# A gated layer whose first two token groups are computed by halves of the hidden units, with 13 instead of 20 weight pieces prepared inside the experts' runs

## The chip, the cores and the metric

The kernel runs on one core of one Trainium2 chip. The metric is the time of one execution on the device in microseconds (us). In the rows of the profile PE is TensorE (its matmuls), PEld its weight loads, DVE is VectorE, ACT is ScalarE, POOL is GpSimd, and SP is the engine that only issues transfers here.

## The reference

Three layers follow each other on 4 x 768 = 3072 tokens of 320 features, all in float32 (the weights of the third layer arrive as float64). The first is an attention with a recurrent state, the second a mixture of 8 experts with one expert per token, the third a gated layer over all tokens:

```
h = np.maximum(x[mask] @ w1[e], 0.0)              # expert e: 320 -> 1024
out[mask] = gate_w[mask, None] * (h @ w2[e])      # 1024 -> 320
...
gate = 1.0 / (1.0 + np.exp(-(x @ w_gate)))        # 320 -> 1536
val = x @ w_val                                   # 320 -> 1536
return (gate * val @ w_out).astype(np.float32)    # 1536 -> 320
```

## The kernel before

Each matrix product is made of parts: a number is split into a high part (rounded for the matmul's format, written by ACT) and a low part (the rest, a subtraction), and the products high x high, high x low and low x high are added up in PSUM. The order of all instructions is written out by hand; every engine works off its own queue in that order.

**The experts.** They are done in nine runs over columns of tokens: runs 0 and 1 are expert 0 (256 + 256 columns), runs 2 to 8 are the other seven with 512, 480, 448, 416, 384, 352 and 336 columns. A run has 8 steps f, one for each block of 128 hidden units (`expert_run`). In a step PE makes the first product of block f (8 matmuls into `h_ps`), ACT writes its high part `hh`, DVE its low part `hl` (L1014, L1015), and PE makes the second product of block f - 2 (8 matmuls into `y_ps`, L935 to L940), which needs `hh` and `hl` of that block. At the end of a run PE transposes the token rows of the next run (`tp_m`, L912) in three parts, each of which ACT and DVE turn into `xh` and `xl` (L210); the transposes have two banks of PSUM. Meanwhile (`expert_steps`) POOL and ACT split the next expert's weights, and three further kinds of work are hung into the steps of runs 2 to 8:

- **weight pieces of the gated layer** (`glu_piece`, `f64_load`, `f64_split`): w_gate and w_val are cut into 20 pieces of 128 rows x 384 units: for each of four stretches of 384 units (three blocks of 128) two of w_gate, two of w_val, and one that holds the last 64 rows of both. A piece is loaded by SP into one of two buffers `raw`, and turned from float64 to a high and a low part: on DVE L1076, L1079, L1082, then (after an ACT instruction, L1085) L1086, L1089 and L1071, which is done twice for the pieces of the last 64 rows (`wgs`, `wvs`). A step with an even f takes up a piece: its first three DVE instructions stand behind step f, the others behind step f + 1. `piece_load` puts the next load into SP's queue when a piece is done.
- **deferred small work** (`defer`): one instruction per step, for offsets, places of the output rows, and flags (`flag_ops`).
- `scale_rows`: the gate weights.

**The gated layer.** 6 groups of 512 tokens (g) times 12 blocks of 128 units (f) are 72 tiles, done group by group. Tile t: PE makes gate and value of (g, f) (`gated_l1`: 16 matmuls with 512 columns, into two of the banks 0, 1, 2, 6); ACT takes the sigmoid (L1527), DVE multiplies (`sgm`, L1528), ACT writes the high part `hh` (L1530), POOL the low part `hl` (L1532); and PE makes the output product of tile t - 2 (`gated_l2`: 12 matmuls with 320 columns into `o_ps`, banks 3, 4, 5, 7, which add up over the 12 blocks of a group). Behind the last tile of a group ACT and DVE copy the four banks out (`gated_out`, L1556, L1558) and POOL scatters them to the output. The layer's 12 pieces of w_out (`wo_load`, 128 x 320) are prepared in the tiles 0 to 11, one each; `due` numbers say before which tile a piece must stand in the queues at the latest (`piece_due`). `group_x` splits the tokens of the next group.

Of the kernel before, what the change touches and what calls it, by code (L numbers as in the profile page):

```python
# [15 lines left out]
ALU = mybir.AluOpType  # L16
# [6 lines left out]
def kernel(  # L23
# [30 lines left out]
    G4 = 4  # L54
# [26 lines left out]
    def tp_ps(name):  # L81
        return next_bank((6, 7), name)
# [1112 lines left out]
    def flag_ops():  # L1195

        v = nc.vector
        fl = const.tile([P, 5], F32, name="fl")
        fb = const.tile([P, 1], BF16, name="fb_")
        ok = const.tile([P, 2, NTILE], F32, name="ok")  # L1200
        we = const.tile([P, 3, NE], F32, name="we")
        z = lambda j: fl[:, j:j + 1]
        ps = {}
        ss = v.tensor_single_scalar

        def total():
            ps[0] = tp_ps("fl_ps")
            nc.tensor.matmul(ps[0][:, 0:1], ones_bf, fb, start=True, stop=True)

        def of_expert(u):  # L1210
            return [
                lambda: v.tensor_tensor(
                    out=vm, in0=pick.rearrange("p k e -> p e k"), in1=by_k(win[:, u]), op=ALU.mult
                ),
                lambda: v.tensor_reduce(out=we[:, u], in_=vm, axis=AX.X, op=ALU.add),
            ]

        return of_expert(0) + of_expert(1) + [
            lambda: v.tensor_tensor(out=we[:, 2], in0=cnt, in1=we[:, 0], op=ALU.is_gt),
            lambda: v.tensor_reduce(out=z(4), in_=we[:, 2], axis=AX.X, op=ALU.max),  # L1220
            lambda: v.tensor_reduce(out=z(3), in_=cnt, axis=AX.X, op=ALU.add),
        ] + block_ops(cnt) + [
            lambda: v.tensor_copy(we[:, 0], nblk),
            lambda: v.tensor_tensor(out=nblk, in0=we[:, 0], in1=we[:, 2], op=ALU.mult),
            lambda: v.tensor_reduce(
                out=z(0), in_=ri_all.rearrange("p c s -> p (c s)"), axis=AX.X, op=ALU.max
            ),
            lambda: ss(out=z(0), in_=z(0), scalar=RLIM, op=ALU.is_gt),
            lambda: ss(out=ok[:, 0], in_=ssq, scalar=1e-9, op=ALU.is_ge),
            lambda: ss(out=ok[:, 1], in_=ssq, scalar=1e30, op=ALU.is_le),  # L1230
            lambda: v.tensor_tensor(out=ok[:, 0], in0=ok[:, 0], in1=ok[:, 1], op=ALU.mult),
            lambda: v.tensor_reduce(out=z(1), in_=ok[:, 0], axis=AX.X, op=ALU.add),
            lambda: ss(out=z(1), in_=z(1), scalar=float(NTILE), op=ALU.is_lt),
            lambda: v.tensor_tensor(out=fb, in0=z(0), in1=z(1), op=ALU.add),
            total,
            lambda: v.tensor_scalar(
                out=z(2), in0=z(3), scalar1=float(NT), scalar2=None, op0=ALU.not_equal
            ),
            lambda: v.tensor_tensor(out=z(2), in0=ps[0][:, 0:1], in1=z(2), op=ALU.add),
            lambda: v.tensor_scalar_min(z(2), z(2), 1.0),  # L1240
            lambda: v.tensor_tensor(out=flags[:, 0:1], in0=z(4), in1=z(2), op=ALU.max),
            lambda: v.tensor_copy(flags[:, 1:2], z(2)),
            lambda: v.tensor_scalar(out=z(2), in0=z(2), scalar1=-1.0, scalar2=1.0, op0=ALU.mult, op1=ALU.add),
            lambda: v.tensor_scalar_mul(nlow, we[:, 1], z(2)),
        ]


    last_part = []

    def expert_steps(n):  # L1250

        k = runs[n][0]
        more = n + 1 < len(runs)
        run_ = expert_run(n)

        acts, rest, ends, loads = ([[] for _ in range(NF1)] for _ in range(4))

        def refill(f, u, e, p, lo=None):

            if e < NE:  # L1260
                copies, lows = (split_w1, split_w2)[u](e, p, lo)
                acts[f] += copies
                rest[f].append(lows)
                e, p = (e, p + 2) if p < 2 else (e + 1, p - 2)
                if e < NE:
                    loads[f].append(lambda: (load_w1, load_w2)[u](e, p))

        def prepare(f):
            if n == 1:
                if f % 2:  # L1270
                    refill(f, 0, 1, f // 2)
                elif f == 4:
                    refill(f, 1, 1, 0, nc.vector)
            else:
                if blanks:
                    acts[f].append(blanks.pop(0))
                if f % 2:
                    refill(f, 1, k + f // 4, (f // 2 + 2) % 4)
                elif f or k > 1:
                    refill(f, 0, k + (f > 0), (f // 2 + 3) % 4)  # L1280
                else:
                    refill(f, 1, 1, 1, nc.vector)
                rest[f].append(defer[0:1])
                del defer[0:1]
                if f % 2 == 0:
                    acts[f] += last_part
                    a, b, c, last_part[:] = piece() if (f == 4 if n == 2 else f < 6 or n < 5) else ([],) * 4
                    rest[f].append(a)
                    acts[f + 1] += b
                    ends[f + 1] += c  # L1290
            if 3 <= f < 7 and n > 1 and more:
                acts[f] = scale_rows(n + 1)[f - 3:f - 2] + acts[f]
            if f == 6 and n == 2:
                acts[f] += diag_ops(n)
            if f == 2 and n == 2:
                acts[f] += diag_ops(0) + diag_ops(1)
            if f == 4 and n == 2:
                ends[f].append(scale_first)

        for f in range(NF1):  # L1300
            next(run_)
            if f == 0 and more:
                load_x(n + 1)
            prepare(f)
            if n == 1:
# [12 lines left out]
        return run_
# [126 lines left out]
            for c0 in range(0, F2, NW)  # L1445
        ), key=lambda z: (z[2], z[1]),
    )
    todo = [(z[2] // P, lambda z=z: glu_piece(*z)) for z in todo]
    ready = []

    def piece_load():
        if todo:
            due, load = todo.pop(0)
            ready.append((due, load()))

# [34 lines left out]
    piece_load()  # L1490
    piece_load()
    blanks = [blank(j) for j in range(8)]
    defer = offset_ops() + place_ops() + flag_ops()

    for n in range(2, len(runs)):
        next(expert_steps(n), None)
    weave(last_part)


    NG = NTILE // G4  # L1500
    last = NG * NF2 - 1
    wo = {}

# [8 lines left out]
        return lambda: f64_split(t, DM, [(whole, wo[f][0])], [(whole, wo[f][1])])  # L1512

    load_wo()
    todo += [(f + 2, lambda f=f: wo_load(f)) for f in range(NF2)]
    todo.sort(key=lambda z: z[0])
    while len(ready) < 2:
        piece_load()
    hs, os_ = {}, {}

    def gated_l1(t):
        g, f = t // NF2, t % NF2
        pg, pv = (next_bank((0, 1, 2, 6), nm) for nm in ("g_ps", "v_ps"))
        l1_tile(pg, glu["wg"], xg[g], f)
        l1_tile(pv, glu["wv"], xg[g], f)
# [6 lines left out]
        e.tensor_tensor(out=gl, in0=s, in1=gh, op=ALU.subtract)  # L1532
        hs[t] = (gh, gl)

    def gated_l2(t, js):
        g, f = t // NF2, t % NF2
        if f == 0:
            os_[g] = [bank(j, "o_ps") for j in (3, 4, 5, 7)]
        gh, gl = hs[t]
        wh, wl = wo[f]  # L1540
        for j in js:
            o = os_[g][j][:, 0:DM]
            ts_ = slice(j * P, (j + 1) * P)
            nc.tensor.matmul(o, gh[:, ts_], wh, start=(f == 0), stop=False)  # L1544
            nc.tensor.matmul(o, gh[:, ts_], wl, start=False, stop=False)  # L1545
            nc.tensor.matmul(o, gl[:, ts_], wh, start=False, stop=(f == NF2 - 1))  # L1546

    ot = {}
    puts = []

    def gated_out(g, js):
        if g not in ot:
            ot[g] = wp.tile([P, G4, DM], F32, tag="xrow", name="ot")
        for j in js:
            if j % 2 == 0:
# [10 lines left out]
            puts.append(put)  # L1566

    allj = range(G4)
    for t in range(NG * NF2):
        g, f = t // NF2, t % NF2  # L1570
        piece_due(t)
        gated_l1(t)
        if t >= 2:
            gated_l2(t - 2, allj)
            if (t - 2) % NF2 == NF2 - 1:
                gated_out(g - 1, allj)
        weave(defer[0:4], *piece())
        del defer[0:4]
        if g + 1 < NG and f in (4, 6, 8):
            group_x(g + 1, f // 2 - 2)  # L1580
# [374 lines left out]
```

## Time and profile before

| | us |
|---|---|
| median of 3 runs (780.58 to 780.76) | 780.74 |
| the profiled execution | 783.19 |
| its span, from the first to the last instruction | 781.5 |
| run 2 begins / run 3 begins | 192.95 / 225.35 |
| run 8 ends and the first gated tile begins | 383.33 |
| PE busy (share of the span) | 742.0 (95%) |
| DVE / ACT / POOL busy | 408.5 / 339.4 / 398.8 |

The beginnings of runs and tiles are the starts of their first matmul (L922) in the trace. The shares are averages over stages with different limits; what a stage waits for is read from the stage.

### The profile page before, as it was taken

The page shows a single profiled execution, that of the slowest core. Times are in us where ns is not written, and L with a number is a line of the kernel's source. Part 1 is how long each engine was busy: PE and PEld are TensorE (multiplying, and loading weights), DVE is VectorE, ACT ScalarE, POOL GpSimd, SP SyncE. Part 2 cuts the span into 40 slices and gives each one's busy share as a digit, 9 for nine tenths or more (in the row PEclk, how much of TensorE's full clock was granted, in tenths as well). Part 3 has the DMA queues.
Part 4 walks back from the last instruction along what each step waited for, and adds up shares of the span by engine and source line. Part 5 has one row for each costly group of instructions (what it writes and reads, how often), then busy time and mean ns, then how long its engine had stood idle before and what let it go on. Part 6 is the DMA issues. An engine that isn't in the chain of part 4 may idle for free.

```text
span 781.5 us, 13677 instructions
## 1 busy us (share of the span) xinstructions
PE 742.0 (95%) x5013; PEld 669.1 (86%) x5013; DVE 408.5 (52%) x858; ACT 339.4 (43%) x689; POOL 398.8 (51%) x449
## 2 busy tenths in 40 slices
PE   6789998999999999999999999999999999999995
PEld 5689997998778889998888888888888888888885
DVE  6888888777679889999676611111111111111111
ACT  5765554544866566765444422222222222222221
POOL 6677776647577668786323243342324324324222
PEclk9999999589999999999999999999999999999998
DMA  7555764444445566654022110000000000000001
GB/s 240 172 152 158 237 190 153 138 116 142 153 138 171 156 183 194 183 181 125 21 69 68 34 35 1 1 29 5 1 1 34 0 1 34 1 1 34 1 1 37
DMA packets 39846, 70.19 MB, mean 90 GB/s; under 512 B 4818, under 2 KB 28460, under 8 KB 39772
## 3 DMA queue, kind: packets, MB, share of 16 engines
q1 hardware_dynamic: 36764, 59.61, 25.5%
q0 software_dynamic: 3008, 9.64, 3.9%
q8 instruction: 41, 0.67, 0.3%
q14 instruction: 33, 0.27, 0.1%
HBM read 60.55 MB, written 8.68 MB: 89 GB/s over the span
## 4 chain that ended last, share of the span: by engine, by line
PE 61%; DVE 15%; issue 4%; ACT 1%; DMA 1%; POOL 1%; POOLq 0%; DVEq 0%; ACTq 0%
PE o_ps L1546 5%; PE o_ps L1545 5%; PE o_ps L1544 5%; PE g_ps L922 4%; PE g_ps L923 4%; PE g_ps L924 4%; PE v_ps L923 4%; PE v_ps L922 4%; PE v_ps L924 4%; DVE hl L1015 3%; PE v_ps L926 2%; PE v_ps L925 2%; PE g_ps L925 2%; PE g_ps L926 2%; DVE fa L1089 2%
## 5 line engine op out<-in xcount | busy, mean ns | idle before, releaser
L1532 POOL TENSOR_TENSOR hl<-sgm,hh 128x512 fp32r<-128x512 f32 x71 | 91.9, 1295 | 245.2 <-ACT hh L1530 245.1
L1528 DVE TENSOR_TENSOR sgm<-v_ps,sgm 128x512 f32<-128x512 f32 x72 | 49.8, 691 | 280.6 <-PE v_ps L926 275.2
L1530 ACT CAST hh<-sgm 128x512 fp32r<-128x512 f32 x72 | 44.7, 621 | 136.1 <-DVE sgm L1528 136.1
L1527 ACT ACTIVATE sgm<-g_ps 128x512 f32<-128x512 f32 x72 | 43.0, 597 | 122.6 <-PE g_ps L926 122.5
L1546 PE MATMUL o_ps<-wo,hl 128*128 128x320 f32 x288 | 89.0, 309 | 0.0
L1545 PE MATMUL o_ps<-wo,hh 128*128 128x320 f32 x288 | 88.9, 309 | 0.0
L1544 PE MATMUL o_ps<-wo,hh 128*128 128x320 f32 x288 | 88.6, 308 | 0.0
L429 PE MATMUL s_ps<-qk 128*128 128x128 f32 (+1 forms) x384 | 53.3, 300 | 5.9 <-DMA qk<-in_qkt_dram 5.3
L1544 PEld LDWEIGHTS o_ps<-wo,hh 128*128 128x128 f32 x288 | 54.1, 188 | 2.7
L1545 PEld LDWEIGHTS o_ps<-wo,hh 128*128 128x128 f32 x288 | 54.1, 188 | 2.7
L234 POOL TENSOR_TENSOR w2l<-w2raw,w2h 128x512 fp32r<-128x512 f32 x28 | 39.5, 1409 | 33.2 <-ACT w2h L232 20.9
L936 PE MATMUL y_ps<-hl,w2h 128*128 128x256 f32 (+7 forms) x144 | 49.7, 345 | 5.5 <-DVE hl L1015 5.3
L429 PEld LDWEIGHTS s_ps<-qk 128*128 128x128 f32 (+1 forms) x384 | 48.5, 209 | 7.2 <-DMA qk<-in_qkt_dram 4.8
L1546 PEld LDWEIGHTS o_ps<-wo,hl 128*128 128x128 f32 x288 | 54.1, 188 | 0.0
L223 POOL TENSOR_TENSOR w1l<-w1raw,w1h 128x512 fp32r<-128x512 f32 x32 | 46.2, 1443 | 10.2 <-ACT w1h L220 8.8
L922 PE MATMUL h_ps<-xh,w1h 128*128 128x256 f32 (+7 forms) x144 | 51.2, 356 | 0.0
L935 PE MATMUL y_ps<-hh,w2h 128*128 128x256 f32 (+7 forms) x144 | 50.2, 349 | 0.0
L924 PE MATMUL h_ps<-xh,w1l 128*128 128x256 f32 (+7 forms) x144 | 49.5, 344 | 0.0
L923 PE MATMUL h_ps<-xl,w1h 128*128 128x256 f32 (+7 forms) x144 | 49.4, 343 | 0.0
L1014 ACT ACTIVATE hh<-h_ps 128x256 fp32r<-128x256 f32 (+7 forms) x72 | 34.9, 487 | 32.7 <-PE h_ps L926 28.6
L937 PE MATMUL y_ps<-hh,w2l 128*128 128x256 f32 (+7 forms) x144 | 48.7, 339 | 0.0
L1015 DVE SCALAR_TENSOR_TENSOR hl<-h_ps,hh 128x256 fp32r<-128x256 f32 (+7 forms) x72 | 39.3, 548 | 13.0 <-ACT hh L1014 12.3
(334 smaller groups left out, 2086.4 us busy)
## 6 DMA issues: line engine op xcount, KB each, us to landing
kv<-in_kvo_dram SPq DMA_DIRECT2D x24, 484.0 KB
w2raw<-in_moe_w_dram SPq DMA_DIRECT2D x32, 320.0 KB
w1raw<-in_moe_w_dram SPq DMA_DIRECT2D x32, 256.0 KB
qk<-in_qkt_dram SPq DMA_DIRECT2D x48, 160.0 KB
xs<-x SPq DMA_DIRECT2D x24, 192.0 KB
w1raw<-in_moe_w_dram SPq DMA_DIRECT2D x64, 64.0 KB
raw<-in_moe_w_out_dram SPq DMA_DIRECT2D x12, 320.0 KB
raw<-in_moe_w_gate_dram SPq DMA_DIRECT2D x8, 384.0 KB
```

The lines of the kernel that those rows point to most:

```text
L429: nc.tensor.matmul(pss[u][:, pr_ * L:(pr_ + 1) * L], qk[i % NQ][rows, 2 * u, pr_, :], qk[i % NQ][rows, 1, pr_, :], start=True, stop=True,)
L922: nc.tensor.matmul(ps, hi[:, kk, fs], h[:, kk], start=(kk == 0), stop=False)
L923: nc.tensor.matmul(ps, hi[:, kk, fs], l[:, kk], start=False, stop=False)
L924: nc.tensor.matmul(ps, lo[:, kk, fs], h[:, kk], start=False, stop=False)
L935: nc.tensor.matmul(ys[d], wh, hh, start=first, stop=False)
L936: nc.tensor.matmul(ys[d], wh, hl, start=False, stop=False)
L1015: nc.vector.scalar_tensor_tensor(out=h[f][1], in0=ps, scalar=0.0, in1=h[f][0], op0=ALU.max, op1=ALU.subtract)
L1528: nc.vector.tensor_tensor(out=s, in0=pv, in1=s, op=ALU.mult)
L1532: e.tensor_tensor(out=gl, in0=s, in1=gh, op=ALU.subtract)
L1544: nc.tensor.matmul(o, gh[:, ts_], wh, start=(f == 0), stop=False)
L1545: nc.tensor.matmul(o, gh[:, ts_], wl, start=False, stop=False)
L1546: nc.tensor.matmul(o, gl[:, ts_], wh, start=False, stop=(f == NF2 - 1))
```

## The change

`PIECES` names the steps that take up a weight piece in each run: 1, 3, 3, 2, 2, 1 and 1 of them in the runs 2 to 8, 13 in all, where before every even step did so (f = 4 alone in run 2; 0, 2, 4, 6 in runs 3 and 4; 0, 2, 4 from run 5 on, until the 20 were done in run 8). `room` keeps the loads to these 13. The other 7 pieces are prepared in the gated layer with the 12 of w_out, one per tile. The first 24 tiles are put in another order (`order2`): blocks 0 to 5 of group 0, blocks 0 to 5 of group 1, blocks 6 to 11 of group 0, blocks 6 to 11 of group 1; a block's first use, and with it the `due` of its pieces, is now read from that order (`when`). The partial sums of the first halves are copied out of PSUM into `yT` (`gated_keep`), and added when the second half is copied out (`gated_out`, now all on DVE for groups 0 and 1). The flags' small instructions go behind tile 24, and `group_x` of groups 1 and 2 is placed anew.

```diff
+    PIECES = ((), (), (4,), (2, 4, 6), (2, 4, 6), (2, 4), (2, 4), (4,), (4,))
...
-                    a, b, c, last_part[:] = piece() if (f == 4 if n == 2 else f < 6 or n < 5) else ([],) * 4
+                    a, b, c, last_part[:] = piece() if f in PIECES[n] else ([],) * 4
...
-    todo = [(z[2] // P, lambda z=z: glu_piece(*z)) for z in todo]
+    NH = NF2 // 2
+    NG = NTILE // G4
+    order2 = [(g, f) for f0 in (0, NH) for g in range(2) for f in range(f0, f0 + NH)]
+    order2 += [(g, f) for g in range(2, NG) for f in range(NF2)]
+    when = {f: order2.index((0, f)) for f in range(NF2)}
+    todo = [(when[z[2] // P], lambda z=z: glu_piece(*z)) for z in todo]
     ready = []
+    room = [sum(len(z) for z in PIECES)]
     def piece_load():
-        if todo:
+        if todo and room[0]:
+            room[0] -= 1
             due, load = todo.pop(0)
             ready.append((due, load()))
...
-    defer = offset_ops() + place_ops() + flag_ops()
+    defer = offset_ops() + place_ops()
...
-    todo += [(f + 2, lambda f=f: wo_load(f)) for f in range(NF2)]
+    todo += [(when[f] + 2, lambda f=f: wo_load(f)) for f in range(NF2)]
...
+    def begins(t):
+        g, f = order2[t]
+        return f == 0 or (g < 2 and f == NH)
+    def ends_(t):
+        return t == last or begins(t + 1)
...
+    def part(g, j):
+        i = g * G4 + j
+        return yT[:, i // 3, i % 3 * DM:(i % 3 + 1) * DM]
+    def gated_keep(g):
+        for j in range(G4):
+            (nc.vector.tensor_copy if j % 2 else nc.scalar.copy)(part(g, j), os_[g][j][:, 0:DM])
...
+            if g < 2:
+                nc.vector.tensor_tensor(out=ot[g][:, j], in0=o, in1=part(g, j), op=ALU.add)
...
+            if ends_(t - 2):
+                g2, f2 = order2[t - 2]
+                (gated_out(g2, allj) if f2 == NF2 - 1 else gated_keep(g2))
+        weave(defer[0:2], *piece())
+        del defer[0:2]
+        if t == 2 * NF2:
+            defer += flag_ops()
+        if t in xsteps:
+            group_x(*xsteps[t])
```

Two places show what this does to DVE's queue. The first is the beginning and middle of run 7 (352 columns), before; `hl` is the low part that PE waits for, `raw_4652` and `raw_4723` are two weight pieces, and `we`, `fl` and `cnt` belong to the flags:

```order
L1015 SCALAR_TENSOR_TENSOR hl<-h_ps,hh 128x352
L1219 TENSOR_TENSOR we<-cnt,we 128x8
L1076 TENSOR_SCALAR fa<-raw_4652 128x384
L1079 TENSOR_SCALAR fc<-raw_4652 128x384
L1082 SCALAR_TENSOR_TENSOR fc<-raw_4652,fc 128x384
L1015 SCALAR_TENSOR_TENSOR hl<-h_ps,hh 128x352
L1220 TENSOR_REDUCE fl<-we 128x1
L1086 SCALAR_TENSOR_TENSOR fb<-raw_4652,fa 128x384
L1089 TENSOR_SCALAR fa<-fb 128x384
L1071 SCALAR_TENSOR_TENSOR wgl<-fc,fa 128x384
L1015 SCALAR_TENSOR_TENSOR hl<-h_ps,hh 128x352
```

The same run on DVE after the change, to its last `hl`:

```order
L1015 SCALAR_TENSOR_TENSOR hl<-h_ps,hh 128x352 x5
L1076 TENSOR_SCALAR fa<-raw_4594 128x384
L1079 TENSOR_SCALAR fc<-raw_4594 128x384
L1082 SCALAR_TENSOR_TENSOR fc<-raw_4594,fc 128x384
L1015 SCALAR_TENSOR_TENSOR hl<-h_ps,hh 128x352
L1086 SCALAR_TENSOR_TENSOR fb<-raw_4594,fa 128x384
L1089 TENSOR_SCALAR fa<-fb 128x384
L1071 SCALAR_TENSOR_TENSOR wvl<-fc,fa 128x384
L1015 SCALAR_TENSOR_TENSOR hl<-h_ps,hh 128x352 x2
```

Five `hl` now stand in a row without a piece between them, one piece of three is left, and the flags' instructions are gone from the run.

The second place is in the gated layer, DVE's queue at the tiles 13 and 14 after the change (`sgm` is the product of a tile, `yT<-o_ps` the copies of the first half's sums of group 1, `wgs` and `wvs` the piece of the last 64 rows of the last stretch of units, `wo` the low part of a piece of w_out):

```order
L1537 TENSOR_TENSOR sgm<-v_ps,sgm 128x512
L1573 COPY yT<-o_ps 128x320 x2
L1076 TENSOR_SCALAR fa<-raw_5844 128x384
L1086 SCALAR_TENSOR_TENSOR fb<-raw_5844,fa 128x384
L1079 TENSOR_SCALAR fc<-raw_5844 128x384
L1089 TENSOR_SCALAR fa<-fb 128x384
L1082 SCALAR_TENSOR_TENSOR fc<-raw_5844,fc 128x384
L1071 SCALAR_TENSOR_TENSOR wgs<-fc,fa 64x384
L1071 SCALAR_TENSOR_TENSOR wvs<-fc,fa 64x384
L1537 TENSOR_TENSOR sgm<-v_ps,sgm 128x512
L1076 TENSOR_SCALAR fa<-raw_5895 128x320
L1086 SCALAR_TENSOR_TENSOR fb<-raw_5895,fa 128x320
```

Before, DVE had at this place, from tile 12 to the end of the second group, only the products and the copies of group 0:

```order
L1528 TENSOR_TENSOR sgm<-v_ps,sgm 128x512 x2
L1558 COPY ot<-o_ps 128x320 x2
L1528 TENSOR_TENSOR sgm<-v_ps,sgm 128x512 x12
L1558 COPY ot<-o_ps 128x320 x2
L1528 TENSOR_TENSOR sgm<-v_ps,sgm 128x512 x12
```

So the copies of a half now stand between a product and a weight piece, and the next product stands behind both.

## Rows read from the trace of the kernel before

**Rows 1.** Busy time of each engine in stretches of the span (windows)

```profile
core 0: us, PE busy (x) PEld busy (x) DVE busy (x) ACT busy (x) POOL busy (x), PEclk, DMA share, GB/s
225.35:383.33 157.98, 151.08 (x823) 139.75 (x822) 142.48 (x230) 97.55 (x201) 111.45 (x105) 1.00 0.54 158
287.51:312.65 25.14, 25.14 (x139) 24.86 (x138) 22.93 (x34) 17.41 (x36) 20.14 (x19) 1.00 0.59 175
338.12:362.08 23.96, 22.29 (x138) 21.45 (x138) 22.44 (x41) 15.67 (x34) 18.96 (x18) 1.00 0.59 178
389.00:448.00 59.00, 59.00 (x304) 51.66 (x303) 41.47 (x89) 25.56 (x50) 19.56 (x15) 1.00 0.19 57
448.00:775.00 327.00, 324.88 (x1691) 286.30 (x1689) 48.10 (x73) 82.84 (x143) 114.35 (x95) 1.00 0.03 12
```

**Rows 2.** Waits of PE's weight loads, 240 to 384 us: total, times, longest

```profile
PEld y_ps L936 <- DVE hl L1015: 4.5, 4, 1.5
PEld tp_m L912 <- DVE xl L210: 3.2, 3, 1.5
PEld pm_ps L1146 <- DVE tf L1182: 0.9, 1, 0.9
PEld pn_ps L1165 <- DVE y L1190: 0.7, 1, 0.7
```

**Rows 3.** Timeline of the end of run 6: start, duration, engine, line

```profile
330.02 0.48 ACT L1014 ACTIVATE hh<-h_ps 128x384 fp32r<-128x384 f32 x1
...
330.80 1.34 DVE L1089 TENSOR_SCALAR fa<-fb 128x384 int32<-128x384 int32 x1
...
332.89 1.54 DVE L1071 SCALAR_TENSOR_TENSOR wvs<-fc,fa 64x384 fp32r<-64x384 int32 x1
334.46 0.56 DVE L1015 SCALAR_TENSOR_TENSOR hl<-h_ps,hh 128x384 fp32r<-128x384 f32 x1
...
335.07 0.19 PEld L936 LDWEIGHTS y_ps<-hl,w2h 128*128 128x128 f32 x1 [1.43 <-DVE hl L1015]
```

**Rows 4.** DVE's instructions of weight pieces in runs 3 to 8 (lines by form)

```profile
L1089 DVE TENSOR_SCALAR fa<-fb 128x384 int32<-128x384 int32 x19 | 17.8, 935 | 0.7
L1086 DVE SCALAR_TENSOR_TENSOR fb<-raw,fa 128x384 int32<-128x384 int32 x19 | 17.3, 910 | 0.0
L1079 DVE TENSOR_SCALAR fc<-raw 128x384 int32<-128x384 int32 x19 | 15.2, 798 | 0.0
L1082 DVE SCALAR_TENSOR_TENSOR fc<-raw,fc 128x384 int32<-128x384 int32 x19 | 11.6, 610 | 0.7
L1076 DVE TENSOR_SCALAR fa<-raw 128x384 int32<-128x384 int32 x19 | 11.6, 610 | 0.0
L1071 DVE SCALAR_TENSOR_TENSOR wvl<-fc,fa 128x384 fp32r<-128x384 int32 x8 | 8.8, 1101 | 0.3
```

**Rows 5.** Timeline of DVE and POOL in one gated tile with a w_out piece

```profile
410.86 0.69 DVE L1528 TENSOR_TENSOR sgm<-v_ps,sgm 128x512 f32<-128x512 f32 x1 [0.94 <-PE v_ps L926]
412.29 1.29 POOL L1532 TENSOR_TENSOR hl<-sgm,hh 128x512 fp32r<-128x512 f32 x1 [1.22 <-ACT hh L1530]
412.70 1.22 DVE L1086 SCALAR_TENSOR_TENSOR fb<-raw,fa 128x320 int32<-128x320 int32 x1 [0.92 <-ACT fa L1085]
414.84 0.49 DVE L1071 SCALAR_TENSOR_TENSOR wo<-fc,fa 128x320 fp32r<-128x320 int32 x1
416.27 0.69 DVE L1528 TENSOR_TENSOR sgm<-v_ps,sgm 128x512 f32<-128x512 f32 x1 [0.94 <-PE v_ps L926]
```

**Rows 6.** Timeline of tile 13, where group 0 is copied out

```profile
450.19 0.39 PE L922 MATMUL g_ps<-xh,wgh 128*128 128x512 f32 x1
453.85 0.30 PE L1544 MATMUL o_ps<-wo,hh 128*128 128x320 f32 x1
454.12 0.69 DVE L1528 TENSOR_TENSOR sgm<-v_ps,sgm 128x512 f32<-128x512 f32 x1 [4.72 <-PE v_ps L926]
455.60 0.39 PE L922 MATMUL g_ps<-xh,wgh 128*128 128x512 f32 x1
455.80 0.49 DVE L1558 COPY ot<-o_ps 128x320 f32<-128x320 f32 x1 [0.39 <-PE o_ps L1546]
```

More of the change, by code (lines that the diff above doesn't have):

```diff
@@ L1206, in total @@
         def total():
-            ps[0] = tp_ps("fl_ps")
+            ps[0] = next_bank((0, 1, 2, 6), "fl_ps")
             nc.tensor.matmul(ps[0][:, 0:1], ones_bf, fb, start=True, stop=True)
@@ L1497 @@
     weave(last_part)
-    NG = NTILE // G4
     last = NG * NF2 - 1
@@ L1514 @@
     load_wo()
-    todo += [(f + 2, lambda f=f: wo_load(f)) for f in range(NF2)]
+    todo += [(when[f] + 2, lambda f=f: wo_load(f)) for f in range(NF2)]
     todo.sort(key=lambda z: z[0])
+    room[0] = len(todo)
     while len(ready) < 2:
@@ L1521, in gated_l1 @@
     def gated_l1(t):
-        g, f = t // NF2, t % NF2
+        g, f = order2[t]
         pg, pv = (next_bank((0, 1, 2, 6), nm) for nm in ("g_ps", "v_ps"))
@@ L1533, in gated_l1 @@
         hs[t] = (gh, gl)
+    def begins(t):
+        g, f = order2[t]
+        return f == 0 or (g < 2 and f == NH)
+    def ends_(t):
+        return t == last or begins(t + 1)
     def gated_l2(t, js):
-        g, f = t // NF2, t % NF2
-        if f == 0:
+        g, f = order2[t]
+        if begins(t):
             os_[g] = [bank(j, "o_ps") for j in (3, 4, 5, 7)]
@@ L1543, in gated_l2 @@
             ts_ = slice(j * P, (j + 1) * P)
-            nc.tensor.matmul(o, gh[:, ts_], wh, start=(f == 0), stop=False)
+            nc.tensor.matmul(o, gh[:, ts_], wh, start=begins(t), stop=False)
             nc.tensor.matmul(o, gh[:, ts_], wl, start=False, stop=False)
-            nc.tensor.matmul(o, gl[:, ts_], wh, start=False, stop=(f == NF2 - 1))
+            nc.tensor.matmul(o, gl[:, ts_], wh, start=False, stop=ends_(t))
     ot = {}
     puts = []
+    def part(g, j):
[4 more added lines that the diff above has]
+            (nc.vector.tensor_copy if j % 2 else nc.scalar.copy)(part(g, j), os_[g][j][:, 0:DM])
     def gated_out(g, js):
@@ L1554, in gated_out @@
         for j in js:
-            if j % 2 == 0:
-                nc.scalar.copy(ot[g][:, j], os_[g][j][:, 0:DM])
+            o = os_[g][j][:, 0:DM]
+            if g < 2:
+                nc.vector.tensor_tensor(out=ot[g][:, j], in0=o, in1=part(g, j), op=ALU.add)
+            elif j % 2 == 0:
+                nc.scalar.copy(ot[g][:, j], o)
             else:
-                nc.vector.tensor_copy(ot[g][:, j], os_[g][j][:, 0:DM])
+                nc.vector.tensor_copy(ot[g][:, j], o)
             i = g * G4 + j
@@ L1568 @@
     allj = range(G4)
+    xsteps = {1 + u: (1, u) for u in range(3)}
+    xsteps.update({order2.index((1, 6)) + 2 * u: (2, u) for u in range(3)})
+    xsteps.update({order2.index((g, 4 + 2 * u)): (g + 1, u) for g in range(2, NG - 1) for u in range(3)})
     for t in range(NG * NF2):
-        g, f = t // NF2, t % NF2
+        g, f = order2[t]
         piece_due(t)
@@ L1574 @@
             gated_l2(t - 2, allj)
[L1575 to L1580, printed above, removed]
+            if ends_(t - 2):
[7 more added lines that the diff above has]
+            group_x(*xsteps[t])
     for j in allj:
```

## Prediction, made before the changed kernel was run

> **What bounds the kernel now.** I read the stages first. In the gated layer PE is the bound: of the 327 us from 448 on it is counted busy for 324.88, while DVE works 48.10 [rows 1], and a tile lasts exactly what its matmuls last, 450.19 to 455.60, that is 5.41 us: 3.66 for the first product, then the output product [rows 6]. DVE idles before each product there and waits for PE [rows 5, 6]. In the runs 3 to 8 it is the other way round: DVE is busy 142.48 of 157.98 us [rows 1]. Only the weight loads tell what that costs, because a matmul that waits behind its predecessor is hardly seen: in run 7 PE is counted busy for 22.29 of 23.96 us. The waits of the weight loads name DVE every time: from 240 us on 4.5 us for the low part `hl`, 3.2 for the low part `xl` of the next run's tokens, 0.9 and 0.7 for two small transposes of the places, 9.3 us together [rows 2]. Run 5 has none of them: PE is busy there for 25.14 of 25.14 us [rows 1]. Without late low parts PE itself sets the pace of a run.
>
> Why DVE is late is seen at the end of run 6. ACT has `hh` of block 6 ready at 330.50; DVE begins its `hl` at 334.46, almost 4.0 us later, since it is in the middle of a weight piece (L1089 with 1.34, L1071 with 1.54), and PE stands for 1.43 us [rows 3].
>
> **What leaves the runs.** A weight piece costs DVE there .610 + .798 + .610 + .910 + .935 + 1.101 = 4.96 us on average [rows 4]. Seven go from the runs 3 to 8, one each from 3 to 6, two from 7, one from 8: 35 us of DVE's work, of 142. The piece at f = 0 goes in every run from 3 on. It is the one that hurts: the first two steps have only the first product, so PE is through them quickly, and DVE, just back from the end of the run before, falls behind and carries the lateness through the run. `hl` has two steps of room; with a piece less before it, `hl` of block 6 in run 6 comes some 3 to 5 us earlier and is not late at all (about 2.5 us would do: 4.0 late cost 1.43).
>
> I take the waits one by one. Of the 4.5 us for `hl` (1.43 in run 6, the others in runs 7 and 8, which keep one piece each) all goes. The 0.9 and 0.7 for the places depend on small DVE instructions that stand behind the first pieces of runs 3 and 6; I keep 0.2. Of the 3.2 for `xl`, 0.9 in run 7 goes; the 1.5 and 0.8 at the ends of runs 3 and 4 stand behind the piece taken up at f = 6, which stays: DVE comes to it about a microsecond earlier, so I keep 0.7 and 0.4. Back come 9.3 - 1.3 = **8.0 us**. What is late next is nothing I can see: POOL is busy 18.96 of 23.96 us in run 7 and 20.14 of 25.14 in run 5 [rows 1], and run 5 shows that this much of it does not hold PE; ACT is busy for less. The flags' small instructions, which leave the runs 6 to 8, are part of the same lateness and get no term.
>
> **What the gated layer takes on.** PE has the same matmuls in another order, so nothing is added there. The granted clock is 1.00, the 2.4 GHz level, in all these stretches [rows 1], and nothing makes PE emptier.
>
> The seven pieces and twelve of w_out are done one per tile, in the tiles 0 to 18. A tile with a w_out piece has DVE going from 410.86 to 415.33, 4.47 us, and it then waits 0.94 for PE [rows 5]. A piece of 384 instead of 320 columns is longer by 0.4 (a fifth more of what is left of the 4.47 without the product, 0.6, the wait for ACT, 0.9, and POOL's share in L1086, 0.7): 4.9, under 5.41. The pieces of the last 64 rows have one more L1071, 0.6: 5.4, just a tile. So DVE keeps up, with no reserve in those two tiles.
>
> The reserve is used up where `gated_keep` stands: tiles 7 and 13. Its second DVE copy must wait for the end of the output product; at the same place before, it ran from 455.80 to 456.29, 0.69 us into the next tile [rows 6]. The piece behind it is one of the last 64 rows in both tiles: 5.4 less the product's 0.6 is 4.8 us, and it ends 5.5 us into tile 14; the product of tile 14, otherwise 3.93 us into its tile (454.12 [rows 6]), waits for it, and the w_out piece behind that ends 5.5 + 4.5 - 5.4 = 4.6 us into tile 15. The output product that needs this piece begins at 3.7 (its low weights at 3.8). Price: 0.8 us, once, at tile 15; in tile 7 nothing is due so soon. The lower bound is zero: L1086 takes 1.22 us in a tile because POOL's `hl` is running (412.29 to 413.58, and L1086 begins at 412.70) [rows 5]; in tile 13 the piece begins later, when POOL's `hl` is over, and the chain is 0.7 shorter. I take **0.3 us**, nearer to that.
>
> At no cost: the eight copies of the first halves (0.49 each on DVE [rows 6]); the next output product begins 3.66 us into its tile, the banks are free after 0.69. The sums on DVE for groups 0 and 1 stand where no piece follows. `group_x` of group 1 (three conversions on ACT and POOL) comes in tiles 1 to 3, for tile 6; POOL is busy 19.56 of 59 us there [rows 1]. The loads lie a tile and more ahead, with DMA busy 0.19 of the time [rows 1]. `fl_ps` takes a bank of the ring once.
>
> **The sum.** 781.5 - 8.0 + 0.3 = 773.8 us of span. The profiled execution took 783.19, 1.7 more than its span and 2.45 more than the median of 780.74; I take the difference from the median: 780.74 - 7.7 = **773.0 us**.
>
> **The rivals.**
>
> *Only part of the waits goes* (775.6). The waits at the ends of runs 3 and 4 (1.5, 0.8) and for the places (1.6) stay whole: 4.5 + 0.9 back, less 0.3. For it: the piece at f = 6 is still there, and so is most of DVE's load in run 3. Against it: DVE's lateness in those runs begins with the piece that goes. Chance 0.17.
>
> *The load goes to the gated layer and comes due there* (some 783, slower). Its place is tiles 6 to 18, where the queue of DVE would grow from tile to tile, and every piece becomes a wait of PE. It decides at DVE's chain per tile: above 5.41 us each of 13 tiles loses the excess, so the gain is eaten at 5.41 + 8.0 / 13 = 6.0, and the kernel is slower by over 0.2% (1.6 us, about what a measurement of this kernel can tell from no change) from 6.15. At the runs' mean of 4.96 for a piece, with 0.7 for the product and 0.9 of waiting for ACT, the chain would be 6.5 for 384 columns; at some 6.2 in the mean it costs 10 us: 780.7 - 8 + 10 = 783. Against it: POOL, beside which these instructions get long, is busy a third of the time here instead of over two thirds [rows 1]. Chance 0.06. The Trainium skill (SBUF — State Buffer, Who interferes with whom) states that DVE instructions with two SBUF inputs or in a two-port mode and POOL's instructions exclude each other for a whole instruction; that is the sharing that this rival needs, and rows 5 agree for L1086.
>
> *No gain* (781). PE is counted busy for 151.08 of 157.98 us in the runs [rows 1]; if the weight loads' waits were only shifted within PE's queue, 0.3 would be lost and nothing won. Against it: the pause of 1.43 in rows 3 is followed by no catching up. Chance 0.05.
>
> *More than the waits* (764). If the runs could go at the density of run 5, where weight loads fill 24.86 of 25.14 us, their 139.75 us of loads would take 141.3: 16.7 back [rows 1]. Against it: a weight load lasts 0.19, but matmuls of 512 columns follow at 3.66 / 16 = 0.23 [rows 6], so wide runs cannot be as dense. Chance 0.03. The Trainium skill (Perfetto Trace Analysis, Identifying the Most-Contended Engine) has TensorE's headroom judged by the weight loads' busy share rather than the matmuls'; by that alone the sum would be 780.7 - 16.7 + 0.3 = 764.3, and I expect the trace to side with the column count.
>
> The forecast has the remaining 0.69; its own range is 771.4 (all 9.3 back, nothing paid) to 774.5 (7.0 back, 0.8 paid).
>
> **Numbers.** The range for 8 in 10 takes the forecast and the first rival with their bounds: at best all 9.3 and nothing paid, 771.4, which I round down to 771.0; at worst 4.5 + 0.9 back, and 0.8 paid with as much again in a second place, 776.9, rounded to 777.0. Faster by over 0.2%: 0.69 + 0.17 + 0.03, less a little for the unseen, 0.88. Within 0.2%: 0.05. Slower: 0.07.
>
> **What would show it.** Right: in runs 6 to 8 no wait of the weight loads for `hl`; run 7 near 21.5 us and run 8 near 19.8; the gated layer starts some 8 us earlier and its 72 tiles last as before, but for a pause under 1 us near tile 15. Wrong: products on DVE (L1537) that start later from tile to tile between 6 and 18, or PE waiting there for `wg`, `wv` or `wo`; or waits of the same sum in the runs that name ACT or POOL.

## The result and the profile after

| | before | after |
|---|---|---|
| median, us | 780.66 (780.16 to 780.76, 4 runs) | 773.72 (772.58 to 774.3, 4 runs) |
| ratio | | 0.9909 (95%: 0.9884 to 0.9933) |
| span of the profiled execution, us | 781.5 | 770.9 |
| start of run 2 in it | 192.95 | 190.54 |
| run 2 | 32.40 | 31.97 |
| runs 3 to 8 | 157.98 | 149.78 |
| gated layer to the end | 398.15 | 398.58 |

The forecast was 773.0 (771.0 to 777.0). The two profiled spans differ by 10.6 us, the medians by 6.9. The four last rows of the table say why: 2.4 of it lies ahead of run 2, where both kernels issue the same work. In ten profiled executions of before, after and the variants below, run 2 began anywhere between 190.54 and 194.69. What the change does is read from the stretches behind that: 8.20 us less in the runs 3 to 8, 0.43 more in the gated layer, net 7.77. The interval of the ratio, 5.2 to 9.1 us, holds it. Stretches in which PE has no wait repeat far better than the total (run 5 took 25.10 or 25.13 us in all eight kernels that have two pieces in it), so the experiments are read by the stretches. Where there are waits, a run can differ by 0.2 to 0.5 us between two kernels that issue the same work in it, as the first experiment shows.

The windows of the kernel after, for the runs 3, 4, 5 and 7 and for 3 to 8 together (columns as in [rows 1]):

```profile
222.51:253.53 31.02, 30.66 (x143) 25.47 (x142) 27.27 (x41) 17.41 (x34) 20.16 (x21) 1.00 0.56 157
253.53:282.42 28.89, 28.23 (x142) 25.29 (x140) 24.29 (x34) 18.01 (x36) 20.72 (x21) 1.00 0.59 170
282.42:307.52 25.10, 25.10 (x139) 24.86 (x138) 18.57 (x27) 15.92 (x33) 18.68 (x19) 1.00 0.58 170
331.09:352.66 21.57, 21.57 (x138) 21.53 (x138) 13.05 (x21) 13.91 (x30) 17.84 (x18) 1.00 0.47 141
222.51:372.29 149.78, 148.76 (x824) 140.00 (x822) 113.03 (x166) 90.34 (x185) 106.43 (x105) 1.00 0.51 148
```

DVE went from 142.48 to 113.03 us of work, 29.5 less, and the stretch became 8.2 shorter. The prediction had 35 us for the seven pieces; the 29.5 even hold the flags' instructions, and the instructions of the pieces that stayed got longer (L1076 and L1082 0.88 and 0.90 us in the mean, 0.61 before [rows 4]). Run 7 went from 23.96 to 21.57, and PE's weight loads now fill 21.53 of it: PE waits for nothing there any more. Run 5 lost a piece too (DVE 22.93 to 18.57) and gained nothing (25.14 to 25.10), since PE had no wait in it before.

The waits of PE's weight loads from 230 to 373 us of the kernel after (total, times, longest), against [rows 2]:

```profile
PEld tp_m L912 <- DVE xl L210: 1.0, 1, 1.0
PEld tp_m L912 <- issue: 0.7, 4, 0.2
PEld tp_m L912 <- ACT w2h L232: 0.3, 2, 0.2
PEld pn_ps L1165 <- DVE hl L1015: 0.2, 1, 0.2
```

The four waits for `hl` are gone, and of 9.3 us that named DVE 1.2 are left: 1.0 at the end of run 4 and 0.2 in run 6. The two lines that name `issue` and ACT stand in the kernel before with the same 0.7 and 0.3.

The tiles of the gated layer last 5.41 us as before, except tile 15 (5.72) and the tiles 35 and 36 (5.45 and 5.51); tiles 0 to 2 and the last have other lengths in both kernels, and differ between them by 0.11 us or less. DVE's timeline from the end of tile 13, which begins at 439.01, to tile 15, which begins at 449.83 (start, duration):

```profile
442.94 0.69 DVE L1537 TENSOR_TENSOR sgm<-v_ps,sgm 128x512 f32<-128x512 f32 x1 [0.67 <-PE v_ps L926]
...
444.62 0.49 DVE L1573 COPY yT<-o_ps 128x320 f32<-128x320 f32 x1 [0.39 <-PE o_ps L1562]
...
446.55 0.56 DVE L1086 SCALAR_TENSOR_TENSOR fb<-raw,fa 128x384 int32<-128x384 int32 x1 [0.68 <-ACT fa L1085]
...
448.74 0.56 DVE L1071 SCALAR_TENSOR_TENSOR wvs<-fc,fa 64x384 fp32r<-64x384 int32 x1
449.32 0.69 DVE L1537 TENSOR_TENSOR sgm<-v_ps,sgm 128x512 f32<-128x512 f32 x1
...
453.28 0.49 DVE L1071 SCALAR_TENSOR_TENSOR wo<-fc,fa 128x320 fp32r<-128x320 int32 x1
```

and PE's weight loads in tile 15:

```profile
453.83 0.19 PEld L1561 LDWEIGHTS o_ps<-wo,hh 128*128 128x128 f32 x1 [0.39 <-DVE wo L1071]
```

That is the chain of the prediction, link by link: the kept copy waits for the output product, the piece of the last 64 rows follows it, the product of tile 14 starts 4.90 us into its tile instead of 3.92, and the w_out piece of tile 14 is ready 3.94 us into tile 15, where PE wanted it 0.39 us sooner.

### The profile page after: what moved, and what is told of

Read it like the earlier page. It is cut to its first block, busy times and chain, and to the rows that moved or that the text cites. A ratio compares the mean times of both kernels' runs of the same rounds, so it can differ in the third digit from the quotient of the medians.

```text
span 770.9 us, 13685 instructions
## 1 busy us (share of the span) xinstructions
PE 737.4 (96%) x5013; PEld 667.9 (87%) x5013; DVE 408.8 (53%) x866; ACT 340.0 (44%) x689; POOL 393.3 (51%) x449
## 5 line engine op out<-in xcount | busy, mean ns | idle before, releaser
L223 POOL TENSOR_TENSOR w1l<-w1raw,w1h 128x512 fp32r<-128x512 f32 x32 | 44.4, 1386 | 14.2 <-ACT w1h L220 12.5
L234 POOL TENSOR_TENSOR w2l<-w2raw,w2h 128x512 fp32r<-128x512 f32 x28 | 36.8, 1316 | 23.6 <-ACT w2h L232 18.7
```

## The experiments

All of them are the changed kernel with the edit shown. The ratios are against the kernel before as it ran beside them: beside the kernels with twenty pieces, with thirteen from f = 0 on, with fifteen at the old places and with the plain order it took 782.78 us (median), beside the other four 781.41.

**Twenty pieces in the runs, the gated layer by halves.**

```diff
-    PIECES = ((), (), (4,), (2, 4, 6), (2, 4, 6), (2, 4), (2, 4), (4,), (4,))
+    PIECES = ((), (), (4,), (0, 2, 4, 6), (0, 2, 4, 6), (0, 2, 4), (0, 2, 4), (0, 2, 4), (0, 2))
```

> The changed kernel with 20 pieces in the experts' runs again (at the places of before) and the gated layer still by halves. Theory, the whole gain comes from the pieces that leave the runs: runs 3 to 8 take about 157 us again (149.8 in the changed kernel, 158.0 before), the waits for hl in runs 6 to 8 and for xl are back, the gated layer loses nothing at tile 15 because its w_out pieces stand seven tiles earlier, and the time is that of before, 780.7 (779.5 to 781.2). Rival, the order by halves or the later flags bring part of it: runs 3 to 8 stay under 155 us, or the gated layer is shorter than before, and the time is 774 to 778.

780.08 us, ratio 0.9957 (0.9939 to 0.9975). The runs 3 to 8 took 155.98 us, the gated layer 398.16 with no pause at tile 15. The waits of the weight loads in the runs (from 222 us on, so with one of 0.8 for `hl` at the start of run 3 that every kernel here has; the lines that name DVE):

```profile
PEld y_ps L936 <- DVE hl L1015: 4.7, 6, 1.2
PEld tp_m L912 <- DVE xl L210: 2.6, 2, 1.5
PEld pn_ps L1165 <- DVE y L1190: 0.7, 1, 0.7
PEld pm_ps L1146 <- DVE tf L1182: 0.7, 1, 0.7
```

The waits are back with the pieces, and the gated layer is as long as before: the order by halves brings no time itself. But 2.0 of the 8.2 us came without any piece being moved, 1.8 of them in runs 7 and 8 (22.79 and 20.63 instead of 23.96 and 21.25). The difference there is the flags, which this kernel still has behind the runs. So the rival is right in part. The theory's 157 was about 1 us too high, and the time is below that of before by 2.7 us (2.0 to 4.8), not the same. The 2.0 is read from one trace of each kernel: the runs 3 to 5, in which both issue the same work, differ by 0.28 and 0.20 us one way and 0.50 the other.

**The flags back in the runs.**

```diff
-    defer = offset_ops() + place_ops()
+    defer = offset_ops() + place_ops() + flag_ops()
...
-        if t == 2 * NF2:
-            defer += flag_ops()
```

> The changed kernel with the flags' small instructions of DVE back in the experts' runs, one behind each block from run 6 or so on, as before. In the kernel with 20 pieces the runs 3 to 8 took 156.0 us and not 158.0, 1.8 of the difference in runs 7 and 8, so the flags were worth about 2 there. Theory, DVE has slack now: with two pieces and one piece a run the flags cost nothing, runs 3 to 8 take 149.8 us within 0.4, and the time is that of the changed kernel, 0.991 of before. Rival, the flags have a price of their own: about 2 us come back, in runs 7 and 8, and the ratio is 0.9935.

774.03 us, ratio 0.9900 (0.9871 to 0.9928). Every run took what it takes in the changed kernel within 0.01, 149.78 us together. So the flags cost about 2 us beside twenty pieces and nothing beside thirteen: the two parts of the change remove the same lateness, and either one's worth depends on the other. The tiles 35 and 36 were 5.41 here, so their 0.04 and 0.10 us are the price of the flags in the gated layer (tile 36 of the changed kernel begins right behind the flags' one matmul, L1208).

**Thirteen pieces, but from f = 0 on.**

```diff
+    PIECES = ((), (), (4,), (0, 2, 4), (0, 2, 4), (0, 2), (0, 2), (0,), (0,))
```

> Thirteen pieces in the runs as in the changed kernel, but each run's pieces begin at f = 0 instead of f = 2 (or 4). Theory, the place decides: the piece at f = 0 makes the hl of the first blocks late, PE waits for hl again in runs 6 to 8, runs 3 to 8 take 152 to 156 us, and the time is 776 to 780. Rival, only the number of pieces decides: runs 3 to 8 take 149.8 us within 0.7, the time is 773.7 within 0.7.

775.52 us, ratio 0.9904 (0.9880 to 0.9928). The runs 3 to 8 took 149.68 us: the rival was right and the theory fell. The waits from 222 us on:

```profile
PEld y_ps L936 <- DVE hl L1015: 1.0, 2, 0.8
PEld tp_m L912 <- issue: 1.0, 6, 0.2
PEld pm_ps L1146 <- DVE tf L1182: 0.6, 1, 0.6
PEld pn_ps L1165 <- DVE y L1190: 0.3, 1, 0.3
```

By run the places do differ, but in both directions: run 3 took 31.43 (31.02 in the changed kernel) and run 6 23.91 (23.58), which lose 0.3 to 0.4 by the piece at f = 0; run 4 took 28.01 (28.89), since without the piece at f = 6 its `xl` is not late. Runs 7 and 8 are the same to 0.01 with their only piece at 0 or at 4.

**Only the pieces at f = 0 leave; fifteen stay.**

```diff
+    PIECES = ((), (), (4,), (2, 4, 6), (2, 4, 6), (2, 4), (2, 4), (2, 4), (2, 4))
```

> Only the pieces at f = 0 leave the runs (and run 8 keeps two): 15 pieces stay instead of 13, runs 7 and 8 have two each, at f = 2 and 4. Theory, the place decides: no wait for hl in runs 7 and 8, runs 3 to 8 take 149.8 us within 0.7; the w_out pieces come two tiles earlier, so the pause of 0.31 us at tile 15 is gone; the time is 773.4 (772.8 to 774.0). Rival, the number decides: two of seven pieces are back, so some 2 of the 8.2 us as well, 775.7.

776.88 us, ratio 0.9914 (0.9889 to 0.9938), which cannot tell it from the changed kernel; the stretches can. Runs 3 to 8 took 151.23 us, run 7 22.48 and run 8 20.15, 1.4 more than with one piece each; the pause at tile 15 is gone (398.19). The waits of the weight loads in runs 7 and 8:

```profile
PEld y_ps L936 <- DVE hl L1015: 1.4, 2, 0.9
```

DVE's timeline in run 7, the first and the last instruction of both pieces and the low parts behind them:

```profile
339.25 0.35 DVE L1076 TENSOR_SCALAR fa<-raw 128x384 int32<-128x384 int32 x1
...
344.84 1.54 DVE L1071 SCALAR_TENSOR_TENSOR wvl<-fc,fa 128x384 fp32r<-128x384 int32 x1
346.31 0.51 DVE L1015 SCALAR_TENSOR_TENSOR hl<-h_ps,hh 128x352 fp32r<-128x352 f32 x1
346.74 1.43 DVE L1076 TENSOR_SCALAR fa<-raw 128x384 int32<-128x384 int32 x1
...
351.86 1.53 DVE L1071 SCALAR_TENSOR_TENSOR wgl<-fc,fa 128x384 fp32r<-128x384 int32 x1
353.31 0.94 DVE L1015 SCALAR_TENSOR_TENSOR hl<-h_ps,hh 128x352 fp32r<-128x352 f32 x2
```

DVE goes without a pause from 339.25 to 353.39: two pieces and the low parts between them need 14.1 us, and the four steps for which they were planned last 4 x 2.58 = 10.3 (2.58 us is one step of run 7 without a wait). The second piece starts late by what the first ran over, and the low parts of the last blocks pay. Neither place alone nor number alone says this; what is planned for neighbouring steps does.

**Fifteen pieces with steps between them.**

```diff
+    PIECES = ((), (), (4,), (2, 4, 6), (0, 2, 4), (2, 4), (2, 4), (0, 4), (0, 4))
```

> Fifteen pieces in the runs, but with steps between them: runs 7 and 8 take theirs at f = 0 and 4 instead of 2 and 4, and run 4 at 0, 2, 4 instead of 2, 4, 6. Theory, the density decides: in run 7 a step lasts 2.58 us, two pieces in four steps are more than DVE can do beside the low parts, two in six are not; run 7 takes 21.6 us and not 22.5, run 8 19.6 and not 20.15, run 4 28.0 and not 28.9; runs 3 to 8 take 148.9 (148.6 to 149.5), and no pause is left at tile 15 (gated layer 398.2); together 1.2 us less than the changed kernel. Rival, the number decides: runs 7 and 8 keep the 1.4 us that they lost with two pieces each, and runs 3 to 8 take 150.4.

772.37 us, ratio 0.9878 (0.9854 to 0.9901). Runs 3 to 8 took 148.92 us, run 7 21.57, run 8 19.62, run 4 28.01; the gated layer 398.14. All as the theory had it. The last piece of runs 7 and 8 stands at f = 4 as in the kernel before this one; only the first moved away from it. DVE in run 7 now has a pause between the two:

```profile
335.61 0.35 DVE L1076 TENSOR_SCALAR fa<-raw 128x384 int32<-128x384 int32 x1
...
341.21 0.94 DVE L1015 SCALAR_TENSOR_TENSOR hl<-h_ps,hh 128x352 fp32r<-128x352 f32 x2
342.62 0.53 DVE L1015 SCALAR_TENSOR_TENSOR hl<-h_ps,hh 128x352 fp32r<-128x352 f32 x1 [0.47 <-ACT hh L1014]
343.06 0.42 DVE L1076 TENSOR_SCALAR fa<-raw 128x384 int32<-128x384 int32 x1
...
349.47 0.51 DVE L1015 SCALAR_TENSOR_TENSOR hl<-h_ps,hh 128x352 fp32r<-128x352 f32 x1
```

This version beats before in time, and the changed kernel by 1.3 us in the stretches (148.92 + 398.14 against 149.78 + 398.58). In time it was 772.37 against 774.03 for the kernel with the flags back, which has the changed kernel's stretches; the intervals of the two ratios overlap, so the time alone does not show the 1.3.

**Thirteen pieces, the gated layer in the order of before.**

```diff
-    order2 = [(g, f) for f0 in (0, NH) for g in range(2) for f in range(f0, f0 + NH)]
-    order2 += [(g, f) for g in range(2, NG) for f in range(NF2)]
+    order2 = [(g, f) for g in range(NG) for f in range(NF2)]
...
-        return f == 0 or (g < 2 and f == NH)
+        return f == 0
...
-            if g < 2:
-                nc.vector.tensor_tensor(out=ot[g][:, j], in0=o, in1=part(g, j), op=ALU.add)
-            elif j % 2 == 0:
+            if j % 2 == 0:
...
-    xsteps = {1 + u: (1, u) for u in range(3)}
-    xsteps.update({order2.index((1, 6)) + 2 * u: (2, u) for u in range(3)})
-    xsteps.update({order2.index((g, 4 + 2 * u)): (g + 1, u) for g in range(2, NG - 1) for u in range(3)})
+    xsteps = {order2.index((g, 4 + 2 * u)): (g + 1, u) for g in range(NG - 1) for u in range(3)}
```

> Thirteen pieces in the runs, but the gated layer in the order of before: all 12 units of group 0, then group 1, nothing kept. Then all 20 + 12 pieces are due by tile 13, 14 of the 19 that are left before the first product of tile 9. Theory, DVE's chain of 4.5 to 5.4 us for a piece is the limit of the gated layer: some 14 pieces of 4.15 us and 9 products of 0.6 against 45 us until tile 9, PE stands some 18 us, the time is 792 (785 to 800), slower than before. Rival, the gated layer has room for the pieces in either order: 774 to 776.

794.96 us, ratio 1.0157 (1.0125 to 1.0189). The runs took 149.86 us, so the gain is there; the tiles 6, 8 and 9 took 9.09, 7.62 and 20.22, and the gated layer 418.88, 20.7 more than before. The waits of the weight loads in the gated layer:

```profile
PEld g_ps L922 <- ACT wgh L1068: 8.1, 2, 5.8
PEld g_ps L925 <- ACT wvs L1068: 7.8, 2, 5.6
PEld g_ps L924 <- DVE wgl L1071: 0.8, 1, 0.8
```

A window within tile 9 (columns as in [rows 1]):

```profile
430.00:440.00 10.00, 3.67 (x8) 2.50 (x9) 8.97 (x22) 4.05 (x9) 0.00 (x0) 0.50 0.46 135
```

The waits name the weights, and DVE works 8.97 of 10 us. That is the prediction's rival on the slower side, with its mechanism. The waits add up to 16.7 of the 20.7 us; in the rest the clock has a part, since the granted clock was 0.50 in this window and 0.57 from 406 to 410. The halves gain nothing by themselves (the first experiment); they push the due times of half the units six tiles back, and only that makes it free to move the pieces.

**More work for DVE in the tiles 6 to 18.**

```diff
+    fx = cv.tile([P, 160], I32, tag="fx", name="fx")
+    nc.vector.memset(fx, 0)
+
+    def extra():
+        nc.vector.tensor_single_scalar(out=fx, in_=fx, scalar=0x7FFFFFFF, op=ALU.bitwise_and)
...
         weave(defer[0:2], *piece())
+        for _ in range(7 if 6 <= t <= 18 else 0):
+            extra()
```

> The changed kernel with seven more DVE instructions (128x160, some 1.2 us together, on a tile that nothing else reads) behind the piece in each of the tiles 6 to 18. Theory, DVE's chain has a reserve of 0.9 us in a tile with a w_out piece, 0.5 with 384 columns, none with the last 64 rows: the chains become 5.7, 6.1 and 6.6 against 5.41, the lateness adds up to some 8 us by tile 18, PE waits for it from about tile 14 on when the w_out pieces come due a tile later, the gated layer takes 405 us (402 to 408) instead of 398.6, and the time is some 6 us above the changed kernel's. Rival, DVE has more room than its chain shows: the layer takes under 400 us.

786.61 us, ratio 1.0063 (1.0046 to 1.0081); the gated layer took 410.61 us, 12.0 more than in the changed kernel and above the 402 to 408 of the theory. The seven instructions took more than planned: they begin at 446.84 and the product behind them at 448.66, so they add 1.82 us and not 1.2. The waits of the weight loads in the layer:

```profile
PEld o_ps L1560 <- ACT yT L1573: 4.8, 1, 4.8
PEld o_ps L1561 <- DVE wo L1071: 3.6, 5, 0.7
PEld o_ps L1560 <- ACT wo L1068: 2.0, 5, 1.2
```

PE began to wait at tile 14, as the theory had it. But the way in which the layer got longer is not the one of the prediction's rival, by which each tile loses its excess. No tile before 14 was longer than 5.41 us, although the product came late in every one from tile 7 on: 6.89 us into tile 8, 10.86 into tile 12, 13.86 into tile 14, against 3.92. Then tile 14 took 11.59, tile 15 8.48, and the tiles 16 to 19 6.20 or 6.21 each. So lateness is stored for some eight tiles at no price, and is paid at once when the copies of group 1's first half, which stand behind the late `hh` on ACT, hold the banks that the next output product needs. From then on the w_out pieces are due a tile later, and each tile lasts as long as DVE's chain. That chain can be read here: 6.20 - 1.82 = 4.38 us with a w_out piece, and with 384 columns from one product to the next 455.12 - 448.66 = 6.46, less 1.82, 4.64. The two products, from DVE's timeline:

```profile
448.66 0.68 DVE L1537 TENSOR_TENSOR sgm<-v_ps,sgm 128x512 f32<-128x512 f32 x1
...
455.12 0.68 DVE L1537 TENSOR_TENSOR sgm<-v_ps,sgm 128x512 f32<-128x512 f32 x1
```

**The kept copies inside the piece.**

```diff
-                (gated_out(g2, allj) if f2 == NF2 - 1 else gated_keep(g2))
-        weave(defer[0:2], *piece())
+                if f2 == NF2 - 1:
+                    gated_out(g2, allj)
+        a, b, c, d = piece()
+        weave(defer[0:2], a, b)
+        if t >= 2 and ends_(t - 2) and order2[t - 2][1] < NF2 - 1:
+            gated_keep(order2[t - 2][0])
+        weave(c, d)
```

> The changed kernel with the copies of the first halves taken into the piece, between its first three DVE instructions and its ACT instruction on one side and the rest on the other, so that the wait for the output product lies where DVE waits for ACT anyway. Theory, the copies make the piece late, the piece the product of the next tile and the w_out piece of tile 15: the products of tiles 8 and 14 start at 3.93 into their tile and not 4.9, the pause of 0.31 us at tile 15 is gone, and the gated layer takes 398.2 us instead of 398.6. Rival, the piece of the last 64 rows is too long by itself: the product of tile 14 is late by 0.3 or more and the pause stays.

773.86 us, a single execution; the gated layer took 398.18 us, tile 15 5.41, and no weight load waits between 380 and 560. DVE from tile 13 on:

```profile
445.88 0.56 DVE L1082 SCALAR_TENSOR_TENSOR fc<-raw,fc 128x384 int32<-128x384 int32 x1
446.36 0.88 DVE L1573 COPY yT<-o_ps 128x320 f32<-128x320 f32 x2
447.16 0.86 DVE L1086 SCALAR_TENSOR_TENSOR fb<-raw,fa 128x384 int32<-128x384 int32 x1
...
450.02 0.69 DVE L1537 TENSOR_TENSOR sgm<-v_ps,sgm 128x512 f32<-128x512 f32 x1 [0.43 <-PE v_ps L926]
```

The product waits for PE again, 0.43 us with nothing else to do, and the pause is gone. But the edit does two things. It takes the copies' wait (0.39 us) out of DVE's way, and it also runs a piece's first three DVE instructions in one go, in every tile, so that most of DVE's wait for ACT goes too (0.68 us in tile 14 of the changed kernel, none here). This version alone does not part the two. The kernel of the experiment with steps between the pieces, which has the changed kernel's order of instructions, does: there the piece of the last 64 rows follows no copies, and the product behind it, at 439.28, starts 3.92 us into tile 12, on time; the copies in front of an ordinary piece make the product of tile 8 late by 0.29 us (at 417.94, 4.21 into its tile); copies and the piece of 64 rows together make it 0.97 or 0.98 late in the changed kernel. The products of the tiles 8 and 12 in the kernel with steps between the pieces:

```profile
417.94 0.69 DVE L1537 TENSOR_TENSOR sgm<-v_ps,sgm 128x512 f32<-128x512 f32 x1
...
438.62 0.56 DVE L1071 SCALAR_TENSOR_TENSOR wvs<-fc,fa 64x384 fp32r<-64x384 int32 x1
439.28 0.69 DVE L1537 TENSOR_TENSOR sgm<-v_ps,sgm 128x512 f32<-128x512 f32 x1
```

So the piece of 64 rows just fits by itself, and the lateness needs the copies in front of it. 0.4 us is too little for a measurement of the time to show; the traces show it.

## Why the prediction was right, step by step

*What comes back in the runs* (8.0): 8.20 us. Of the 9.3 us of waits 1.2 are left, where 1.3 were forecast: 0.2 for the places as written, and 1.0 for `xl`, but differently spread. The wait at the end of run 3 (1.5) went altogether, and so did the 0.9 for the places; the one at the end of run 4 stayed (0.8 before, 1.0 now), and goes only when the piece at f = 6 does, as run 4 showed when its pieces began at f = 0. Run 7 took 21.57 (about 21.5), run 8 19.62 (19.8). Run by run the fit is looser: in run 3 waits of 2.46 us went and the run became 2.05 shorter; in run 4 the wait grew by 0.25 and the run became 0.20 shorter all the same. A step of run 4 took 3.31 us before and 3.24 after, with no wait in either, and 3.24 in the kernel with twenty pieces too; why is not known. The two misfits cancel, so that 8.20 comes as near to 8.0 as it does is luck in part.

*Why the pieces hurt*: here the reason was wrong, though the sum was right. The prediction said of the piece at f = 0 that "It is the one that hurts". With thirteen pieces from f = 0 on the runs took the same time, and with only the pieces at f = 0 taken out (and run 8 left with two) they got back 6.75 us and not 8. The sum came out because it was taken from the waits and not from the place. What the runs show in its place: in run 7 a piece with the low parts beside it occupies DVE for 5.7 to 7.1 us, two steps are 5.2, and the overrun adds up over neighbouring pieces until the low parts of the last blocks are late. Two pieces with free steps between them do no harm there, whether one of them stands at f = 0 or not. In run 5 two steps are 6.02 us, and three pieces in a row just fit (25.14 before) or just don't (25.64 in the kernel with twenty).

*The flags* ("part of the same lateness and get no term"): right for this kernel, 0.00 us in the runs. Beside twenty pieces they are worth about 2.0.

*The gated layer* (0.3, between 0 and 0.8): 0.31 at tile 15, by the links given, with the piece on the short side of the two bounds: `L1086` took 0.56 us at 446.55, after POOL's `hl`, so the w_out piece was ready 3.94 us into the tile and not 4.6. The tiles 35 and 36 add 0.15 by the flags, which was not foreseen; the first three tiles, which the flags have left, and the last one make up the difference to 0.43. DVE's chain was put 0.1 to 0.3 too high (4.47 and 4.9; 4.38 and 4.64 measured under load), so the reserve was a little larger than stated.

*The sum*: 7.77 us by the stretches, 7.7 forecast. The median fell by 6.9; its interval, 5.2 to 9.1, holds the 7.7.

*The rivals.* "Only part of the waits goes" was wrong on the ends of the runs but for 1.0 us in run 4. "The load comes due in the gated layer" did not happen, but it does happen in the two kernels that were made for it (794.96 in the plain order, 786.61 with 1.82 us more per tile). Its break-even was mis-stated: not every tile above 5.41 loses its excess; lateness is first stored and then paid at once. The sum was still near (13 tiles at an excess of 0.8 to 1.1, 10 to 14 us; 12.0 measured). "No gain" fell with the first row of the runs. "More than the waits" (764) fell too: the weight loads fill 24.86 of 25.10 us in run 5 and 21.53 of 21.57 in run 7, but in runs 3 and 4 only 25.47 of 31.02 and 25.29 of 28.89, of which waits are some 1.6 and 1.5 us. A step of 16 matmuls without a wait took 3.47, 3.24, 3.01, 2.77, 2.58 and 2.45 us in the runs 3 to 8, so it goes with the columns (480 to 336) in all of them; the loads, 0.19 us each, look full where the matmuls follow each other in less than that. The Trainium skill (Perfetto Trace Analysis, Identifying the Most-Contended Engine) names MFU and the busy share of the weight loads as the measures of TensorE's headroom. The trace does not agree with the second alone: by it the runs 3 and 4 would have 5.5 and 3.6 us of headroom, where the waits leave some 1.6 and 1.5.

## What to carry to other kernels

When filler work is moved from a stage that waits to one that does not, the gain is the waits that go in the stage it leaves, not the work moved (29.5 us of DVE's work left the runs, 8.2 were gained), and two edits that remove the same lateness must not be added up. Place filler by what an engine has to do in each two or three neighbouring steps against the length of those steps; the same number of pieces with free steps between them cost nothing, where side by side they cost 1.4 us. Before moving such work to a stage with due times, work out for each due time what must be done by then: it was the order by halves, which saves nothing itself, that turned a loss of 12 us into a gain of 7.

## What the runs showed of the hardware

The same DVE instruction took 1.24 or 0.56 us, by whether POOL's `hl` was running. In the kernel after, POOL's two `hl` around tile 13:

```profile
438.95 1.29 POOL L1541 TENSOR_TENSOR hl<-sgm,hh 128x512 fp32r<-128x512 f32 x1 [4.11 <-ACT hh L1539]
444.36 1.29 POOL L1541 TENSOR_TENSOR hl<-sgm,hh 128x512 fp32r<-128x512 f32 x1 [4.11 <-ACT hh L1539]
```

and `L1086` beside the first of them:

```profile
439.43 1.24 DVE L1086 SCALAR_TENSOR_TENSOR fb<-raw,fa 128x384 int32<-128x384 int32 x1 [0.94 <-ACT fa L1085]
```

At 446.55, after the second had ended, it took 0.56. The Trainium skill (SBUF — State Buffer, Who interferes with whom) states the exclusion of DVE's and POOL's instructions on a shared port; these rows agree with it.

Pauses of PE were followed by a lower clock. With the extra load PE stood for 4.4 us ahead of 456.84, and the granted clock was 0.50 (the 1.2 GHz level) in the 5.9 us behind it; the windows of that kernel before, in and behind the pause:

```profile
440.50:450.00 9.50, 9.50 (x52) 8.40 (x51) 7.72 (x23) 2.77 (x6) 1.29 (x1) 1.00 0.31 85
450.00:456.80 6.80, 2.42 (x11) 1.69 (x9) 6.01 (x16) 2.49 (x6) 1.56 (x2) 0.94 0.17 48
456.80:462.70 5.90, 5.86 (x18) 5.35 (x19) 4.81 (x15) 2.34 (x5) 1.21 (x1) 0.50 0.19 56
```

At half the clock 5.9 us do the work of 2.95. How much of that is in the 12.0 us stays open, since the next output product waited for its w_out piece anyway. In the kernel in plain order shorter pauses were followed by the same: behind one of 1.84 us, which ended at 405.74, the granted clock was 0.50 from 407 to 409, and behind one of 2.05 us, which ended at 424.47, and one of 0.34 soon after, it was 0.50 from 427 on, through two more pauses of 5.44 and 4.86 us, to 443. The waits of up to 1.5 us in the runs left the clock at 1.00 [rows 1].
